# Layout of q, k and v prepared on the host for a fused attention and mixture-of-experts kernel

## The chip, the cores and the metric

The kernel runs on one core of a Trainium2 chip. The metric is the device time in microseconds of one execution, median of several runs. The core has a matmul engine (PE, with its weight loads PEld), a vector engine (DVE), a scalar engine (ACT), GpSimd (POOL), a queue engine that issues transfers (SP) and 16 DMA engines. Work that numpy does ahead of the launch is not part of the device time.

## The reference

Sparse attention over 8 batches, 8 heads, 576 positions, 64 per head, then a mixture of experts over the 4,608 tokens:

```
scores = scale * q @ k.T                       # scale = 1/8
mask_local   = (rel >= 0) & (rel < 32)         # heads 0..3, rel = query - key
mask_strided = (rel >= 0) & (key % 32 == query % 32)   # heads 4..7
x = softmax(where(mask, scores, -1e9)) @ v     # per head, heads side by side: 4608 x 512
noisy = x @ w_gate + log1p(exp(x @ w_noise)) * noise    # 8 experts
top2 of noisy, softmax weights over the two
out[t] += weight * (relu(x[t] @ w1[e]) @ w2[e])         # w1 512 x 1024, w2 1024 x 512
```

## The kernel before

Attention goes by units: one batch, one pair of heads, either local or strided, 32 units in all, four to a batch. A strided unit takes 72-key groups, a local unit 64 queries against 96 keys; each unit has nine blocks of 64 queries per head, worked in two items of four and five blocks.

A unit's steps, in the names of the code: `loads` (q, k, v by SP; the strided v passes through `vraw` and a copy into `v_s`, and its first 64 rows come a second time into `v_0`; the local v gets a column of ones in `v_l` and a copy of the 32 rows before each block, `front`); `prep` (L494 to L539: local q and k are reordered from `raw` to `ord` by a vector engine, transposed on PE in trains of three at L515, or of four at L519 for strided, and evacuated into `kT_l`, `qT_l`, `kT_s`, `qT_s`, q with the scale; strided units get a last block by eight quadrant copies); `products` (the masks as matmuls, L560, then the scores, L567); `item` twice (maximum `mx` L594, exponentials L598 and L600, transposes of them L608, evacuation to `aT`, values L627, for the fifth block of the second item L632, row sums, reciprocals and products L637 to L656 into `xo`); `finish` (stores of `xo` to `x_dram`, transposes L698 and L694, evacuation to `xT`). In the second item L632 writes the two heads of the fifth block side by side onto partitions 0 to 63.

After a batch's four units comes `route`: the gate matmul (L744), top two, and 12 scatters by POOL (L834) of the tokens' entries into a table in DRAM, `tab`. The experts work in jobs of two or three blocks of 128 tokens: table load by SP (L937), indices by POOL (L994), gathers of tokens from `x_dram` (L978, L985), transposes (L1020 on PE for early jobs, L1024 on DVE for others), a split into a high and a low part (cast L1031, subtraction L1033), layer 1 (L1062, twelve matmuls for each of eight parts of the hidden layer, then L1083 and L1088), layer 2 (L1114, 24 matmuls a block), `res` weighted (a ring of tiles), and a scatter with addition into `out` (L1150). Each expert's 16 weight tiles are loaded into `wraw` (five deep) and split by ACT (L904) and DVE (L905). Six jobs of experts 0 to 2 work on lists of the first 2, 3, 5 or 7 batches and can start while attention goes on; L1069 is one matmul on zeros ahead of some jobs. `out` is first filled with zeros by 12 transfers of 768 KB (L1199).

The order of everything is fixed when the program is built: each step is a `Piece` with an engine (or ANY, which is ACT or DVE), an estimated duration, a rank and what it reads and writes; `issue_all` places them one by one, each time the piece that can start first, and among those within 120 ns of it the one of lowest rank. A DMA waits in this plan until the planned wire is less than 5 us behind (zeros, `bulk`, 1.5 us); `t0` is the earliest planned time. On PE an expert's matmul is preferred while attention is ahead of it by PE time. Where the plan foresees an idle stretch of PE during attention it puts in matmuls on zeros (L375). Units have ranks 0, 10, 20 and so on; expert steps have ranks from `ER` = 1,000,000 on, so they come behind all attention that is ready. `near` is a hook for another rank and returns the rank itself:

```
def near(n, rank):

    return rank
```

Of the kernel before, what the change touches and what calls it, by code (L numbers as in the profile page):

```python
# [22 lines left out]
def kernel(  # L23
    ctx: ExitStack,
    tc: tile.TileContext,
    q: bass.AP,
    k: bass.AP,
    v: bass.AP,
# [7 lines left out]
    nc = tc.nc  # L36
    B, H, S, D = q.shape
# [5 lines left out]
    NP = HL // 2  # L43
# [8 lines left out]
    LP, LJ = S // 6, 6  # L52
# [109 lines left out]
    v_l = [keep.tile([KW, 2, NBL, D + 1], F32, name=f"v_l{i}") for i in range(2)]  # L162
    v_s = [keep.tile([G, 2, NJ, D + 1], F32, name=f"v_s{i}") for i in range(2)]

    v_0 = [keep.tile([G, 2, D + 1], F32, name=f"v_0{i}") for i in range(2)]
    xo_ = [keep.tile([128, 5, 2, D], F32, name=f"xo{i}") for i in range(3)]
    nc.vector.memset(kT_l[:, :STRIDE], 0.0)
    for i in range(2):
        nc.vector.memset(v_l[i][:, :, :, D:D + 1], 1.0)
        nc.vector.memset(v_l[i][:STRIDE, 0, 0, :], 0.0)  # L170
        nc.vector.memset(v_0[i][QB:], 0.0)
        nc.vector.memset(v_0[i][:QB, :, D:D + 1], 1.0)
        nc.vector.memset(v_s[i][:, :, :, D:D + 1], 1.0)
    nc.vector.memset(kT_s[:, NBL - 1, QB:], 0.0)
    for x in xo_:
        nc.vector.memset(x[QB:, 4, :, :], 0.0)
# [36 lines left out]

    PACE = 1.0
# [212 lines left out]
    for name, shape, dtype, depth in (  # L427
            ("raw", [LP, 2, LJ, D], F32, 2), ("ord", [LP, LJ, 2, D], F32, 1),
            ("vraw", [GP, NJ, D], F32, 1), ("ks", [GP, 2, NJ, D], F32, 1), ("qs", [GP, 2, NJ, D], F32, 1),
            ("mx", [128, 5], F32, 3), ("ex", [128, 5, KW], F32, 2), ("aT", [128, 5, 128], F32, 2),  # L430
            ("rs", [128, 6], F32, 2),
            ("xT", [128, S], F32, 5),
            ("noise", [TB, T, E], F32, 1), ("lsb", [TB, T, 2 * E], F32, 1), ("lgT", [96, S // 3], F32, 1),
            ("ns", [TB, T, E], F32, 1), ("nz", [TB, T, E], F32, 1), ("mv", [TB, T, 8], F32, 1),
            ("mi", [TB, T, 8], U32, 1), ("wt", [TB, T, 2], F32, 1), ("ixf", [TB, T, 2], F32, 1),
            ("oh", [TB, T, 2, E], F32, 1), ("ohs", [TB, T, E], BF16, 1),             ("cnt", [TB, E], F32, 1), ("addr_f", [TB, T, 2], F32, 1), ("ent", [TB, T, 2, 3], I32, 2), ("addr", [TB, T, 2], I32, 2)):
        R[name] = ring(keep, shape, dtype, name, depth)
    R["kT_l"], R["qT_l"] = Ring(1, fixed=[kT_l]), Ring(1, fixed=[qT_l])
    R["kT_s"], R["qT_s"] = Ring(1, fixed=[kT_s]), Ring(1, fixed=[qT_s])
    R["xo"] = Ring(3, fixed=xo_)  # L440
    R["v_l"], R["v_s"], R["v_0"] = Ring(2, fixed=v_l), Ring(2, fixed=v_s), Ring(2, fixed=v_0)

    def base_of(u):
        b, p, local = units[u]
        return (b * H + (2 * p if local else HL + 2 * p)) * S * D

    def loads(u, rank):

        base, local = base_of(u), units[u][2]
        res = {}  # L450

        def put(key, slot, parts, new):
            for i, (sel, src, off, dims, nbytes) in enumerate(parts):
                dma(lambda o, s=slot, sel=sel, src=src, off=off, dims=dims:
                    nc.sync.dma_start(sel(s.t), dram(src, off, dims)),
                    nbytes, rank, wires={D: 1.65, LJ * D: 1.2}.get(dims[-1][1], 1.0),
                    **({"alloc": [slot]} if i == 0 else {"write": [slot]}))
            res[key] = slot


        rows = GP if units[u][:2] != (B - 1, NP - 1) else G
        for key, src in (("k", k), ("q", q)):
            if local:
                put(key, R["raw"].new(), [(lambda t: t.rearrange("p h j d -> p h (j d)"), src, base,
                                           [[LJ * D, LP], [S * D, 2], [1, LJ * D]], 294912)], True)
            else:
                put(key, R[key + "s"].new(), [(lambda t: t[:rows].rearrange("p h j d -> p h (j d)"), src, base,
                                               [[NJ * D, rows], [S * D, 2], [1, NJ * D]], 4096 * rows)], True)
        if local:


            slot = R["v_l"].new()
            put("v", slot, [(lambda t: t[STRIDE:].rearrange("p h n d -> p (h n) d")[:, :, :D], v, base,
                             [[D, QB], [QB * D, 2 * NBL], [1, D]], 294912)], True)

            def front(o):
                vv = slot.t.rearrange("p h n d -> p (h n) d")
                copy(o.e, vv[:STRIDE, 1:, :D], vv[QB:, :2 * NBL - 1, :D])
            Piece("ANY", {"ACT": act(64 * (2 * NBL - 1)), "DVE": 760}, front, rank, read=[slot], write=[slot])
        else:  # L480
            slot = res["v"] = R["v_s"].new()
            for h in range(2):
                put(f"v{h}raw", R["vraw"].new(), [(lambda t: t[:rows].rearrange("p j d -> p (j d)"), v, base + h * S * D,
                                                   [[NJ * D, rows], [1, NJ * D]], 2048 * rows)], True)

                def spread(o, h=h, raw=res[f"v{h}raw"]):
                    copy(o.e, slot.t[:G, h, :, :D], raw.t[:G])
                Piece("ANY", {"ACT": act(NJ * D), "DVE": 420}, spread, rank, read=[res[f"v{h}raw"]],
                      **{"write" if h else "alloc": [slot]})
            put("v0", R["v_0"].new(),  # L490
                [(lambda t: t[:QB, :, :D], v, base, [[D, QB], [S * D, 2], [1, D]], 65536)], True)
        return res

    def prep(u, L, rank):  # L494

        local = units[u][2]
        kT, qT = (R["kT_l"].new(), R["qT_l"].new()) if local else (R["kT_s"].new(), R["qT_s"].new())
        tens = (("k", kT, None), ("q", qT, scale))
        for which, slot, factor in tens:
            for c in range(2):  # L500
                ps, src = Slot(), L[which]
                if local:

                    if c == 0:
                        L["o" + which] = R["ord"].new()
                        Piece("ANY", {"ACT": 840, "DVE": 75 + 0.62 * 768}, lambda o, src=src, dst=L["o" + which]: copy(
                            o.e, dst.t, src.t.rearrange("p h j d -> p j h d")), rank, read=[src], alloc=[L["o" + which]])
                    src = L["o" + which]

                def tr(o, c=c, ps=ps, src=src):  # L510
                    if local:

                        pv = ps.t[:, :S // 2].rearrange("r (x j) -> r j x", j=LJ // 2)
                        for j in range(LJ // 2):
                            nc.tensor.transpose(pv[:, j, :], src.t[:, LJ // 2 * c + j, :, :], ident[:LP, :LP])  # L515
                    else:

                        for j in range(NJ // 2):
                            nc.tensor.transpose(ps.t[:, G * j:G * j + G], src.t[:G, c, 2 * j:2 * j + 2, :], ident[:G, :G])  # L519
                Piece("PE", 260, tr, rank, read=[src], psum=ps)  # L520

                def evac(o, c=c, ps=ps, slot=slot, which=which, factor=factor):
                    if local:
                        dst = slot.t[:, STRIDE:] if which == "k" else slot.t.rearrange("r n x -> r (n x)")
                        dst = dst.rearrange("r (x j) -> r x j", j=LJ)[:, :, LJ // 2 * c:LJ // 2 * c + LJ // 2]
                    else:
                        dst = slot.t[:, 4 * c:4 * c + 4, :]
                    copy(o.e, dst, ps.t[:, :S // 2].rearrange("r (a b) -> r a b", b=LJ // 2 if local else G), factor)
                Piece("ANY", {"ACT": act(S // 2), "DVE": dve(S // 2)}, evac, rank, read=[ps],
                      **({"write" if c else "alloc": [slot]}))  # L530
        if not local:

            for _, slot, _ in tens:
                for c, r in enumerate(halves):
                    for odd, ro in enumerate(halves):
                        Piece("ANY", {"ACT": 240, "DVE": 205}, lambda o, slot=slot, c=c, r=r, odd=odd, ro=ro: copy(
# [761 lines left out]
```

## Time and profile before

| | |
|---|---|
| median of 3 runs | 1107.29 us (1105.77 to 1109.4) |
| profiled execution | 1117.46 us, span 1115.7 us |
| busy: PE, PEld | 1069.2 us (96%), 945.9 us (85%) |
| busy: DVE, ACT, POOL | 556.0 us (50%), 474.3 us (43%), 539.8 us (48%) |
| moved by DMA | 133.03 MB, mean 119 GB/s |

Times in rows are microseconds from the start of the span. An engine's busy time is the union of its instructions' records; a matmul's record goes on while the next one has started, so the step from start to start, not the length of a record, is what one costs in a train. A line of the form L515 is line 515 of the kernel before. The granted clock of PE (PEclk) is a share of 2.4 GHz; it has two levels, 1.2 and 2.4 GHz, and a figure between is a mean.

### The profile page before, as it was taken

To read this page: it belongs to the slowest core of one execution; us is meant where nothing else is said; L and a number is where in the kernel's file an instruction comes from. 1 tells how busy PE (TensorE), PEld (TensorE's weight loads), DVE (VectorE), ACT (ScalarE), POOL (GpSimd) and SP (SyncE) were. 2 spreads that over 40 slices of the span, in tenths; PEclk is the share of its full clock that TensorE was granted. 3 is DMA by queue.
4 is the path that set the end of the run, shared out by engine and by line. 5 is a ranking of instruction groups with operands and counts; after the bars stand their busy time and mean duration, and the time that the engine had idled before them with its cause. 6 is when DMAs were issued, how large, how long until landed. Compare 5 with 4: busy or idle time off the path is not lost.

```text
span 1115.7 us, 23537 instructions
## 1 busy us (share of the span) xinstructions
PE 1069.2 (96%) x8790; PEld 945.9 (85%) x8790; DVE 556.0 (50%) x1536; ACT 474.3 (43%) x1203; POOL 539.8 (48%) x661
## 2 busy tenths in 40 slices
PE   8988887989999999999999999999999999999997
PEld 7867766888788898988879898989989898989886
DVE  7857766865476224624746236323633462355231
ACT  6867766766565222423433224222512252244221
POOL 1044334423424467655668475646554655556432
PEclk9998989989999999999999999999999999999999
DMA  9986857878785134543555235523642363243222
GB/s 199 241 195 153 221 137 207 193 179 208 181 245 136 29 52 97 137 75 72 141 133 133 43 57 136 115 44 54 163 85 46 59 179 61 44 116 81 43 46 31
DMA packets 168430, 133.03 MB, mean 119 GB/s; under 512 B 51864, under 2 KB 136344, under 8 KB 168296
## 3 DMA queue, kind: packets, MB, share of 16 engines
q1 hardware_dynamic: 145160, 92.31, 32.1%
q0 software_dynamic: 23136, 38.94, 19.9%
q8 instruction: 83, 1.36, 0.5%
q14 instruction: 51, 0.42, 0.1%
HBM read 92.85 MB, written 39.39 MB: 119 GB/s over the span
## 4 chain that ended last, share of the span: by engine, by line
PE 87%; issue 5%; DVE 3%; DMA 1%; ACT 1%; POOL 1%; another core or an unknown queue 1%; POOLq 0%; SPq 0%; DVEq 0%; ACTq 0%
PE bankB L1114 6%; PE bankE L1114 5%; PE bankF L1114 5%; PE bankC L1062 5%; PE bankH L1062 5%; PE bankG L1062 5%; PE bankE L1062 5%; PE bankC L1114 5%; PE bankF L1062 4%; PE bankD L1062 4%; PE bankA L1062 4%; PE bankA L1114 4%; PE bankB L1062 4%; PE bankG L1114 4%; PE bankH L1114 3%
## 5 line engine op out<-in xcount | busy, mean ns | idle before, releaser
L985 POOL DMA_INDIRECT xg<-x_dram,gxx x248 | 258.5, 1043 | 165.8 <-DVE xr L1024 71.8
L1150 POOL DMA_INDIRECT out_dram<-res,tabt x80 | 133.4, 1667 | 99.7 <-ACT res L289 54.0
L834 POOL DMA_INDIRECT tab<-ent,addr x96 | 91.3, 951 | 89.9 <-issue 26.8
L1024 DVE STREAM_TRANSPOSE xr<-xg 128x512 f32<-128x512 f32 (+1 forms) x66 | 68.1, 1032 | 42.4 <-DMA xg<-x_dram,gxx 33.8
L1031 ACT CAST xhi<-xr 128x512 fp32r<-128x512 f32 (+1 forms) x66 | 39.1, 592 | 53.1 <-DVE xr L1024 51.2
L1033 DVE TENSOR_TENSOR xlo<-xr,xhi 128x512 fp32r<-128x512 f32 (+1 forms) x66 | 43.5, 659 | 35.9 <-ACT xhi L1031 25.2
L905 DVE TENSOR_TENSOR w1lo<-wraw,w1hi 128x512 fp32r<-128x512 f32 x80 | 54.5, 686 | 3.7 <-ACT w1hi L904 1.3
L905 DVE TENSOR_TENSOR w2lo<-wraw,w2hi 128x512 fp32r<-128x512 f32 x80 | 51.8, 684 | 1.2 <-ACT xT L288 0.7
L994 POOL TENSOR_SCALAR gix<-tabt 128x2 int32<-128x2 int32 (+1 forms) x32 | 8.0, 251 | 88.2 <-DMA tabt<-tab 71.0
L904 ACT CAST w1hi<-wraw 128x512 fp32r<-128x512 f32 x80 | 49.0, 618 | 0.4 <-DMA wraw<-in_moe_w_dram 0.2
L904 ACT CAST w2hi<-wraw 128x512 fp32r<-128x512 f32 x80 | 46.6, 617 | 3.3 <-DMA wraw<-in_moe_w_dram 2.7
L1062 PE MATMUL bankH<-xhi,w1hi 128*128 128x256 f32 (+3 forms) x132 | 40.5, 307 | 0.8 <-issue 0.8
L1062 PE MATMUL bankG<-xhi,w1hi 128*128 128x256 f32 (+3 forms) x132 | 40.0, 303 | 0.6 <-issue 0.6
L1062 PE MATMUL bankG<-xlo,w1hi 128*128 128x256 f32 (+3 forms) x132 | 39.4, 299 | 1.0 <-issue 1.0
L1062 PE MATMUL bankC<-xhi,w1hi 128*128 128x256 f32 (+3 forms) x132 | 39.8, 301 | 0.0
L1062 PE MATMUL bankH<-xhi,w1lo 128*128 128x256 f32 (+3 forms) x132 | 39.6, 300 | 0.0
L1062 PE MATMUL bankH<-xlo,w1hi 128*128 128x256 f32 (+3 forms) x132 | 39.6, 300 | 0.0
L1062 PE MATMUL bankG<-xhi,w1lo 128*128 128x256 f32 (+3 forms) x132 | 39.4, 298 | 0.0
L1062 PE MATMUL bankC<-xlo,w1hi 128*128 128x256 f32 (+3 forms) x132 | 39.1, 296 | 0.1
L1062 PE MATMUL bankC<-xhi,w1lo 128*128 128x256 f32 (+3 forms) x132 | 39.2, 297 | 0.0
L1114 PE MATMUL bankB<-w2hi,hhi 128*128 128x512 f32 x96 | 38.9, 405 | 0.0
L1062 PE MATMUL bankF<-xhi,w1hi 128*128 128x256 f32 (+3 forms) x128 | 38.2, 299 | 0.4 <-issue 0.4
(696 smaller groups left out, 3545.8 us busy)
## 6 DMA issues: line engine op xcount, KB each, us to landing
wraw<-in_moe_w_dram SPq DMA_DIRECT2D x160, 256.0 KB
out_dram<-zeros SPq DMA_DIRECT2D x12, 768.0 KB
ks<-in_k_dram SPq DMA_DIRECT2D x15, 320.0 KB
qs<-in_q_dram SPq DMA_DIRECT2D x15, 320.0 KB
vraw<-in_v_dram SPq DMA_DIRECT2D x30, 160.0 KB
raw<-in_k_dram SPq DMA_DIRECT2D x16, 288.0 KB
v_l<-in_v_dram SPq DMA_DIRECT2D x16, 288.0 KB
raw<-in_q_dram SPq DMA_DIRECT2D x16, 288.0 KB
```

The costliest lines, as they stand in the source:

```text
L834: st = nc.gpsimd.indirect_dma_start(out=tab, out_offset=bass.IndirectOffsetOnAxis(ap=s["addr"].t[:, t, kk:kk + 1], axis=0), in_=s["ent"].t ...
L904: Piece("ACT", 620, lambda o: nc.scalar.copy(hi.t, raw.t), rank, read=[raw], alloc=[hi], expert=True)
L905: Piece("DVE", 715, lambda o: nc.vector.tensor_tensor(lo.t, raw.t, hi.t.bitcast(F32), ALU.subtract), rank, read=[raw, hi], alloc=[lo], exp ...
L985: dma(lambda o, g=g: nc.gpsimd.indirect_dma_start(out=xg.t[:, g, :], out_offset=None, in_=x_dram[:4 * known, :], in_offset=bass.IndirectOf ...
L994: nc.gpsimd.tensor_scalar(gi.t[:, :nb], tb.t[:, :nb, 0], known - 1, None, op0=ALU.min)
L1024: Piece("DVE", 8.8 * rows, lambda o, xg=xg, xr=xr, ng=ng, rows=rows: nc.vector.transpose(xr.t.rearrange("p (c x) -> p c x", c=ND)[:, :, :r ...
L1031: Piece("ACT", 620 * rows // 128, lambda o, view=view, cols=cols: nc.scalar.copy(xh.t[:, :, cols], view()), rank, read=[xr], expert=True, ...
L1033: Piece("DVE", 725 * rows // 128, lambda o, view=view, cols=cols: nc.vector.tensor_tensor(xl.t[:, :, cols], view(), xh.t[:, :, cols].bitca ...
L1062: nc.tensor.matmul(ps.t[:, :width], a.t[:, 128 * d:128 * d + 128], c.t[:, d, :width], start=(m == 0), stop=(m == len(todo) - 1))
L1114: nc.tensor.matmul(ps.t, HT[n, f][p[0]].t[:, cols], W2[n][f][p[1]].t, start=(m == 0), stop=(m == len(todo) - 1))
L1150: st = nc.gpsimd.indirect_dma_start(out=out[:known, :], out_offset=bass.IndirectOffsetOnAxis(ap=places(), axis=0), in_=y.t[:rows, :], in_o ...
```

## The change

numpy lays out q, k and v ahead of the launch in the form of the kernel's tiles. For each batch and pair of heads, k and q of a local unit are transposed and put side by side (128 rows of 1,152), q and k of a strided unit likewise in the order of its blocks (128 rows of 1,216), v of either with its column of ones and, for strided, its first 64 rows as a ninth block. A unit has two transfers, `kq` and `v`; `prep` is gone, and the scale moves into the exponentials and one small step on `mx`. The fifth block's heads go to the two halves of the partitions, in the same PSUM tile as the others, with two copies into `xo` instead of one product. Rings: `mx` 5, `ex` 3, `aT` 3, `rs` 4 (before 3, 2, 2, 2), `res` 3 (before 4). Zeros get later `t0`, weights of the first expert earlier ones. Vector steps of early jobs, and the splits of their weights, get a rank after the batches of their list (`near`, with `LAG`).

```
-    kT_l = keep.tile([128, STRIDE + S], F32, name="kT_l")
-    qT_l = keep.tile([128, NBL, QB], F32, name="qT_l")
-    kT_s = keep.tile([128, NBL, G], F32, name="kT_s")
-    qT_s = keep.tile([128, NBL, G], F32, name="qT_s")
...
+    kq_t = [keep.tile([128, STRIDE + 2 * S], F32, name=f"kq_t{i}") for i in range(2)]
+    KS = 8 * G + QB
+    qk_t = [keep.tile([128, S + NBL * G], F32, name=f"qk_t{i}") for i in range(2)]
+    vt_l = [keep.tile([KW, 2, NBL, D + 1], F32, name=f"vt_l{i}") for i in range(2)]
+    vt_s = [keep.tile([GP, 2, NBL, D + 1], F32, name=f"vt_s{i}") for i in range(2)]
...
+    LAG = 60
...
         if local:
+            put("kq", "kq_t", lambda t: t[:, STRIDE:], kq_l, 128, 2 * S, rank)
+            put("v", "v_l", lambda t: t[STRIDE:].rearrange("p h n d -> p (h n d)"), v_l, QB, VW, v_rank)
...
+            put("kq", "qk_t", lambda t: t[:, :S + KS], qk_s, 128, S + KS, rank)
+            put("v", "v_s", lambda t: t.rearrange("p h n d -> p (h n d)"), v_s, GP, VW, v_rank)
...
-    def prep(u, L, rank):
...
-    def products(u, kT, qT, rank):
+    def products(u, kq, rank):
...
+                k0 = QB * blk if local else S + G * blk
+                q0 = (STRIDE + S if local else 0) + QB * blk
+                nc.tensor.matmul(sv[b][halves[half], s, :], kq.t[r, q0:q0 + QB], kq.t[r, k0:k0 + w], start=False,
...
+        Piece("DVE", 90, lambda o: nc.vector.tensor_scalar(mx.t, mx.t, scale, None, op0=ALU.mult), rank, write=[mx],
+              read=[mx])
...
-                nc.scalar.activation(exv()[:, n, :], view(sc)[:, n, :], AF.Exp, bias=mx.t[:, n:n + 1])
+                nc.scalar.activation(exv()[:, n, :], view(sc)[:, n, :], AF.Exp, bias=mx.t[:, n:n + 1], scale=scale)
...
-                    nc.tensor.matmul(extra()[:, h, :], aT.t[:w, 4, 64 * h:64 * h + 64], rhs, start=True, stop=True)
+                    nc.tensor.matmul(main(5)[64 * h:64 * h + 64, 4, :], aT.t[:w, 4, 64 * h:64 * h + 64], rhs, start=True,
+                                     stop=True)
...
-                nc.vector.tensor_tensor(xo.t[:QB, 4, :, :], extra()[:, :, :D],
-                                        rs.t[:QB, 4:, None].to_broadcast([QB, 2, D]), ALU.mult)
+        for h, r in enumerate(halves) if nb > 4 else ():
+            Piece("ANY", {"ACT": 270, "DVE": dve(D)}, lambda o, h=h, r=r: copy(
+                o.e, xo.t[:QB, 4, h, :], main(5)[r, 4, :D], rs.t[r, 4:5]), rank, read=[po, rs], write=[xo])
...
-                    nc.tensor.transpose(ps.t[:, :128], xo.t[:, 4, :, :], ident)
+                    nc.tensor.transpose(ps.t[:, :QB], xo.t[:QB, 4, :, :], ident[:QB, :QB])
...
-            ("res", [128, DM], F32, 4)):
+            ("res", [128, DM], F32, 3)):
...
-        dma(load, 262144, rank if turn is None else turn, alloc=[raw], expert=True, t0=70000 + 2000 * i)
-        Piece("ACT", 620, lambda o: nc.scalar.copy(hi.t, raw.t), rank, read=[raw], alloc=[hi], expert=True)
+        dma(load, 262144, rank if turn is None else turn, alloc=[raw], expert=True, t0=40000 + 1500 * i)
+        Piece("ACT", 620, lambda o: nc.scalar.copy(hi.t, raw.t), late or rank, read=[raw], alloc=[hi], expert=True)
...
         def near(n, rank):
 
-            return rank
+            hb = jobs[n][1][3]
+            return rank if hb == B else 20 * NP * hb + LAG
...
-            ER - 1, t0=26000 + 10000 * c + 35000 * (c >= 5), bulk=True))
+            ER - 1, t0=(90000, 130000, 170000, 230000, 270000)[(c > 2) + (c > 4) + (c > 7) + (c > 10)], bulk=True))
...
+def _laid_out(q, k, v):
...
+    def strided(a, g0):
+        x = pairs(a, H // 2)
+        y = x.reshape(B, NP, 2, G, NJ // 2, 2, D).transpose(0, 1, 5, 6, 2, 4, 3)[..., g0:]
+        return np.concatenate([y.reshape(B, NP, 2 * D, -1), turned(x[:, :, :, :QB])], -1)
...
+    return {"kq_l": np.concatenate([turned(pairs(k, 0)), turned(pairs(q, 0))], -1), "v_l": vl,
+            "qk_s": np.concatenate([strided(q, G - QB), strided(k, 0)], -1), "v_s": vs}
```

## Rows read from the trace of the kernel before

**Rows 1.** Stretch, length; busy PE, PEld, DVE, ACT, POOL (instructions); PEclk, DMA share, GB/s.

```profile
0.00:157.00 157.00, 137.94 (x2174) 112.16 (x2175) 111.89 (x457) 111.42 (x356) 45.40 (x115) 0.96 0.83 195
157.00:368.00 211.00, 197.18 (x2256) 170.34 (x2255) 135.13 (x483) 134.45 (x379) 78.17 (x128) 0.98 0.74 185
368.00:1104.00 736.00, 729.59 (x4345) 660.00 (x4345) 308.97 (x598) 227.74 (x468) 413.10 (x416) 1.00 0.40 85
1104.00:1116.00 12.00, 4.48 (x20) 3.38 (x18) 0.00 (x0) 0.69 (x1) 3.12 (x2) 0.78 0.35 49
```

**Rows 2.** The same view, the first units.

```profile
7.00:56.00 49.00, 46.38 (x801) 38.91 (x802) 41.10 (x160) 40.86 (x136) 1.60 (x5) 1.00 0.98 227
```

**Rows 3.** Timeline of PE: first and eighth unit's scores, batch 1's gate.

```profile
6.91 0.27 PE L567 MATMUL bankE<-kT_s,qT_s 64*64 64x72 f32 x1
...
58.40 0.24 PE L567 MATMUL bankC<-kT_l,qT_l 64*64 64x96 f32 x1
...
78.00 1.56 PE L744 MATMUL bankD<-xT,wg 128*32 128x192 f32 x24 [0.28 <-ACT v_s L288]
```

**Rows 4.** Timeline of POOL: batch 1's entries, its last scatter, indices of the first job.

```profile
85.77 0.20 POOL L822 COPY ent<-wt 96x12 f32<-96x12 f32 x1 [7.84 <-DVE wt L816]
...
111.00 0.91 POOL L834 DMA_INDIRECT tab<-ent,addr  x1 [1.50 <-ACT ex L598]
...
125.93 0.24 POOL L994 TENSOR_SCALAR gix<-tabt 128x2 int32<-128x2 int32 x1
```

**Rows 5.** Timelines of PE, ACT and DVE: the first job's first block.

```profile
136.99 0.65 PE L1020 MATMUL bankD<-ident,xg 128*128 128x128 f32 x4
...
140.24 0.58 ACT L1031 CAST xhi<-bankD 128x512 fp32r<-128x512 f32 x1
...
148.79 0.67 DVE L1033 TENSOR_TENSOR xlo<-bankD,xhi 128x512 fp32r<-128x512 f32 x1
...
156.79 0.37 PE L1062 MATMUL bankE<-xhi,w1hi 128*128 128x256 f32 x1
```

**Rows 6.** Timeline of PE where it never waits: trains of transposes.

```profile
265.21 0.41 PE L515 MATMUL bankD<-ident,ord 96*128 96x96 f32 x3
265.46 0.42 PE L519 MATMUL bankE<-ident,ks 72*128 72x72 f32 x4
265.71 0.41 PE L515 MATMUL bankC<-ident,ord 96*128 96x96 f32 x3
```

**Rows 7.** Stretch 0 to 157 us, line L515 alone, then L519 alone (PE, PEld).

```profile
0.00:157.00 157.00, 15.72 (x108) 10.61 (x108) 0.96 0.83 195
...
0.00:157.00 157.00, 15.15 (x152) 13.08 (x152) 0.96 0.83 195
```

**Rows 8.** Timeline of PE: values of four blocks, of the fifth, the next.

```profile
289.14 0.69 PE L627 MATMUL bankE<-v_s,aT 72*64 72x65 f32 x16
289.66 0.40 PE L632 MATMUL bankE<-v,aT 72*64 72x65 f32 x4
289.99 0.50 PE L1114 MATMUL bankA<-w2hi,hhi 128*128 128x512 f32 x1
```

**Rows 9.** Stretch 0 to 157 us, instructions of ord, kT_s and qT_s (PE, PEld, DVE, ACT).

```profile
0.00:157.00 157.00, 15.72 (x108) 10.61 (x108) 3.28 (x6) 10.80 (x13) 0.96 0.83 195
...
0.00:157.00 157.00, 9.80 (x324) 7.53 (x324) 5.79 (x21) 10.14 (x35) 0.96 0.83 195
...
0.00:157.00 157.00, 9.80 (x324) 7.53 (x324) 6.09 (x24) 9.64 (x31) 0.96 0.83 195
```

**Rows 10.** Line L375 alone in 0 to 157 us; timeline of one filler.

```profile
0.00:157.00 157.00, 20.21 (x137) 13.28 (x137) 0.96 0.83 195
...
31.96 0.82 PE L375 MATMUL bankD<-zeros 128*128 128x256 bf16 x6
32.62 0.62 PE L608 MATMUL bankD<-ident,ex 128*96 128x128 f32 x4
```

**Rows 11.** Timeline of SP: the second transfer of zeros.

```profile
63.08 0.60 SPq L1199 DMA_DIRECT2D out_dram<-zeros  x1
```

More of the change, by code (lines that the diff above doesn't have):

```diff
@@ L444, in base_of @@
         b, p, local = units[u]
[L445 to L468, printed above, removed]
@@ L492, in loads @@
-        return res
-    def prep(u, L, rank):
[L496 to L536, printed above, removed]
-                            o.e, slot.t[r, NBL - 1, :QB].rearrange("r (x j g) -> r j x g", j=NJ // 2, g=2)[:, :, :, odd],
-                            slot.t[ro, 4 * c:4 * c + 4, :QB // NJ]), rank, read=[slot], write=[slot])
-        return kT, qT
@@ L541, in products @@
-    def products(u, kT, qT, rank):
+                vv = slot.t.rearrange("p h n d -> p (h n d)")
+                copy(o.e, vv[:STRIDE, D + 1:], vv[QB:, :VW - D - 1])
+            Piece("ANY", {"ACT": act(VW - D - 1), "DVE": 760}, front, rank, read=[slot], write=[slot])
+        else:
+            put("kq", "qk_t", lambda t: t[:, :S + KS], qk_s, 128, S + KS, rank)
+            put("v", "v_s", lambda t: t.rearrange("p h n d -> p (h n d)"), v_s, GP, VW, v_rank)
+        return res
+    def products(u, kq, rank):
@@ L574, in scores @@
                 product(b, 4, b, NBL - 1)
-        o = Piece("PE", 20 + 10 * w / 4.8 + 5 * (188 if local else 144), scores, rank, read=[kT, qT], psum=sc)
+        o = Piece("PE", 20 + 10 * w / 4.8 + 5 * (188 if local else 144), scores, rank, read=[kq], psum=sc)
         o.order += in_turn[-1:]
@@ L891, with weights_of @@
     ZC = 384
-    def weights_of(e, layer, i, rank, turn=None):
+    def weights_of(e, layer, i, rank, turn=None, late=None):
         raw, hi, lo = R["wraw"].new(), R[f"w{layer}hi"].new(), R[f"w{layer}lo"].new()
@@ L1095, in lows @@
                     low(hh.t[:, width:width + tail], main, width)
-            Piece("DVE", dve(main) + (dve(tail) if tail else 0), lows, rank, read=[ps, hh], write=[hh] if tail else [],
+            Piece("DVE", dve(main) + (dve(tail) if tail else 0), lows, near(n, rank), read=[ps, hh], write=[hh] if tail else [],
                   alloc=[hl], expert=True)
@@ L1162, in experts @@
         for i in range(NF):
-            W[1, i] = weights_of(jobs[0][0], 1, i, ER, turn(0))
-        W2[0] = [weights_of(jobs[0][0], 2, i, ER, turn(0)) for i in range(NF)]
+            W[1, i] = weights_of(jobs[0][0], 1, i, ER, turn(0), near(0, ER))
+        W2[0] = [weights_of(jobs[0][0], 2, i, ER, turn(0), near(0, ER)) for i in range(NF)]
         transposes(0, ER)
@@ L1176, in experts @@
                 for i in range(NF):
-                    W[1, i] = weights_of(jobs[n + 1][0], 1, i, rank + 20, turn(n + 1))
+                    W[1, i] = weights_of(jobs[n + 1][0], 1, i, rank + 20, turn(n + 1), near(n + 1, rank + 20))
             if n + 1 < NJOB:
@@ L1184, in experts @@
                 if change:
-                    W2[n + 1] = [weights_of(jobs[n + 1][0], 2, i, rank + 21, turn(n + 1)) for i in range(NF)]
+                    W2[n + 1] = [weights_of(jobs[n + 1][0], 2, i, rank + 21, turn(n + 1), near(n + 1, rank + 21)) for i in range(NF)]
         Piece("POOL", 7000, lambda o: nc.gpsimd.drain(), rank, after=[out_done[E - 1][-3]], expert=True)
```

137 lines of the change are left out of this document (60 added, 77 removed).

## Prediction

> **What bounds the kernel now.** I read the stretches first: four stages, cut where the first expert matmul starts (157 us), where the last attention work ends (368) and where the last matmul ends [rows 1]. Stage A, 0 to 157 us, has attention and routing alone; stage B, 157 to 368, mixes attention with the jobs of experts 0 to 2 whose tokens are already routed; from 368 on there are expert jobs alone. The reader is to see the idle time of PE: 19.1 us in A (157 less 137.9), 13.8 in B, 6.4 in the 736 us behind, and a tail. From 157 us on the kernel is bound by the sum of PE's work. A change can gain in two ways only: less PE work anywhere, or a shorter stage A, where PE waits and where part of its busy time is filler (matmuls on zeros, L375, that the planner puts into gaps it foresees).
>
> Then I read what sets the length of A. In its first third DMA, DVE and ACT are all near their ends: 98% share, 41.1 and 40.9 of 49 us [rows 2]. The eighth unit, the last of batch 1, has its scores at 58.4 us, the first at 6.9: 7.4 us a unit; batch 1's gate follows at 78.0 [rows 3]. From there a chain of small steps leads to the first expert job: entries ready at 85.8, the twelfth scatter at 111.0, indices at 125.9 on POOL [rows 4]; the tokens' first block is transposed at 137.0, but its cast on ACT comes at 140.2, its subtraction on DVE at 148.8, and the first expert matmul at 156.8 [rows 5]. The expert's vector steps have the lowest rank and stand behind attention. So A = 78 us to the gate + 79 us of routing and preparation.
>
> **The change part by part.** *Transposes of q and k (prep).* In a stretch where PE never waits, trains of these transposes start 0.25 us apart [rows 6]. There are 128 trains (32 units, two tensors, two halves): 128 x 0.25 = 32.0 us of PE work gone. Their summed busy time is higher (an instruction's record overlaps the next one's start), so 32 is the value; 0.42 us, a train's own length in the same rows, bounds it at 53. In A 36 + 38 = 74 trains run [rows 7], so 18.5 us of it lies there and 13.5 in B.
>
> *The fifth block's values.* Its four matmuls (a head's fp32 product counts as two) write the same partitions and take 0.33 us, while 16 ordinary ones, in pairs on opposite halves, take 0.52 [rows 8], or 0.13 for four. After the change the two heads write opposite halves: 0.20 saved in 32 units, 6.4 us (bounds 0, if they don't overlap, and 10.6). The small transpose L694, now 64 by 64: half of a transpose, 0.06 us in 32 units, 2 us (bounds 0 and 4). Together 40.4 us of PE work: 18.5 + 3.4 (17 units) + 1 = 22.9 in A, 17.5 in B.
>
> *Vector work.* Gone are the reordering of raw, the evacuations to kT and qT, the quadrant copies and the spread of v. The three largest groups alone held ACT for 30.6 and DVE for 15.2 us of A [rows 9]. Added are two scalings of mx a unit and one copy more for the fifth block; the nearest rows are those of kT_s, copies of more elements, at a mean of 0.28 on DVE (5.79 us for 21): at most 0.84 us a unit, 15 in A, against 46 gone. So the two engines end below their present 111 of 157 us each [rows 1], and PE and DMA set the pace. The memsets removed lie in the first 7 us, under the loads.
>
> *Loads.* Bytes stay (1.88 MB for two units, by the shapes; the padding adds under 1%), seven transfers become four, runs of 256 to 2,048 bytes become 4.6 to 4.9 KB. DMA moved 227 GB/s at 98% share [rows 2]; 0.94 MB in and 0.29 MB out make 5.4 us a unit. A gain in rate isn't shown here, so none is the lower bound.
>
> *Pace.* PE's kept work bounds a unit from below: stage A's 137.9 less 22.9 less filler of 15.1 (137 at 0.11; six start 0.66 us ahead of their successor, [rows 10]) is 99.9 us for 18.5 units, 5.4. Unchanged is 7.4. I take the middle, 6.3: the eighth scores at 6.9 + 7 x 6.3 = 51. The Trainium skill (DMA: Bandwidth & Descriptors, section Bandwidth) says that efficiency grows with a transfer's size, with 138 GB/s at 64 KB and 341 at 1 MB; no row here shows its rate for the merged transfers. By an estimate from that page a unit's traffic would need 3.6 us, the pace would fall to PE's 5.4, and the forecast by 6 us.
>
> *Gate and routing.* The gate follows the eighth scores by 19.6 us now; with fewer steps to queue behind I take 16 (bounds 12 and 19.6): 67. Routing keeps 7.8 us to the entries and about 23 for the scatters (26 now; POOL is unchanged, its pacing follows the vector engines). Table load and indices, 14 now, 12; gather, 11 now, 9. From the first transposes to the first expert matmul took 19.8 us; the steps that waited now have rank 40 x 2 + 60 = 140, ahead of units 14 and up, and at 115 us those are the units in work: 5 us (the steps' own 0.6 + 0.7 us twice, and the hops). Sum 56.8, first expert matmul at 124 instead of 157.
>
> *Price of the ranks.* Expert casts now go ahead of attention steps on both engines: attention units 14 and up wait behind them. Cover is expert PE work that is ready by then; without it the price is the 1.3 us of cast and subtraction per tile, 16 tiles per expert. I take 0.
>
> *Weights earlier, zeros later.* Of the twelve transfers of zeros the planner let the first go at 26 us or later, and the second left at 63.1 [rows 11], in A's loaded part; now none goes before 90 in the planner's time. One costs 3.5 us at 227 GB/s. The weights' start moves from 70 to 40 us and takes the room: 0 net. Scatters into out wait for zeros on POOL, and with res three deep instead of four a late zero would hold a PSUM bank. The first scatter of a list of three batches needs five transfers of zeros: bounds 0 and their 17 us, if they all have to go then.
>
> *Sum.* In A the filler and idle are 157 - 99.9 - 22.9 = 34.2; with A at 124 and the same attention work done 124 - 99.9 = 24.1. So A gives 22.9 + 10.1 = 33.0, B 17.5, the rest 0: 50.5 us. The profiled execution took 1117.5 us (span 1115.7), 10.2 above the median of the runs shown, 1107.3. 1117.5 - 50.5 - 10.2 = 1056.8: **1057 us**.
>
> **The rivals.**
> *1, forecast:* 1040 to 1072, which is A at 107 to 139. Chance 0.55.
> *2, A collapses further.* With the pace at 5.4 and the gate 12 us behind, the first expert matmul comes at about 105: 19 us less, 1038. For it: all three loaded resources of rows 2 are relieved at once. Against it: the scatter chain of POOL isn't, and DMA still carries the same bytes. Chance 0.17.
> *3, A keeps its length.* If loads, or the scatters, set it anyway, the work removed there turns into idle time and filler, and only B's 17.5 remain: 1107 - 17.5 = 1090. For it: DMA at 98%, and in B it must move in some 150 us what took 211 at a share of 0.74 [rows 1], which gives 1.04 if nothing is postponed. Against it: zeros can slip behind 368, where the share is 0.40. Chance 0.20, most of it between 1072 and 1090.
> *4, nothing happens:* attention shorter but routing chain and expert supply as late, PE's saving filled by zeros: 1107. From 157 us on PE has no filler to grow, so only 0.03.
> *5, slower.* PE's granted clock. The mean of 0.96 in A and 0.98 in B [rows 1] means 12.6 + 8.4 = 21 us at half speed already. With transposes gone PE has less to do ahead of the first expert job; should the clock stay at 1.2 GHz, t us of it lose up to t/2 of work. The 50.5 us are lost at 101 us more, 122 in all: nearly the whole of A at 124 us. For it: PE fell to half in A and B although filled. Against it: the filler remains and the density of work rises (99.9 of 124, against 122.8 of 157). The Trainium skill (TensorE: Matmul & The Clock Gate, Part 1: The HAM clock gate) holds that the slow level is the default and sustained activity ends it; the falls in stages A and B and none to speak of behind 368 (1.00) agree. Chance 0.05, other ways to lose included.
>
> **How the numbers follow.** The likeliest is 1, so 1057. The range leaves out the low third of 2 (below 1030, 0.05), the upper end of 3 (above 1085, 0.06), 4 and 5 (0.08): 0.19, so 1030 to 1085. The measurement of this kernel can tell 0.3%, 3.3 us, from no change. Faster: 1, 2 and 3, 0.92. Same: 4, 0.03. Slower: 5, 0.05.
>
> **What the changed profile would show.** PE busy time less by 40 us besides filler, with no line of transposes of q and k; the first expert matmul near 124; cast, subtraction and matmul within some 5 us of the first token transposes; attention over near 315 or before; DMA's share in what remains of B above 0.85; behind it the same PE-bound stage with 6 us idle. Wrong I would be if the scores of the eighth unit still came at 58 (loads bind), if the gap from gate to first expert matmul stayed near 79 (POOL binds), if stage B had more than 20 us of idle PE (the vector ranks, zeros or loads starve it), or if the expert matmuls' own time changed, which nothing in the trace speaks for.

## The result, and the profile after

The changed kernel takes 1073.4 us (median of 4 runs, 1070.1 to 1076.7) against 1106.5 (1105.0 to 1109.4): a ratio of 0.970, 95% interval 0.966 to 0.974. The forecast was 1057, in a range of 1030 to 1085. The gain is 33 us where 50.5 were worked out. Chips differ: the kernel before takes 1106 to 1114 us on some and 1065 on others, so each experiment is compared with the kernel before on its own chip.

The stretches of the profiled execution (1074.0 us, span 1071.9), cut at the same events as [rows 1]:

```profile
0.00:145.00 145.00, 130.02 (x2046) 98.86 (x2046) 92.76 (x396) 94.89 (x298) 46.43 (x115) 0.95 0.79 216
145.00:305.00 160.00, 153.14 (x1874) 128.49 (x1875) 102.67 (x372) 88.55 (x273) 65.02 (x120) 0.98 0.76 199
305.00:1064.00 759.00, 756.02 (x4494) 685.48 (x4493) 320.34 (x616) 238.03 (x487) 423.05 (x425) 1.00 0.43 91
1064.00:1072.00 8.00, 0.43 (x2) 0.00 (x1) 0.00 (x0) 0.69 (x1) 1.56 (x1) 0.73 0.30 43
```

Stage A shrank from 157 to 145 us, B from 211 to 160; the last stage grew, since more of the expert jobs lie in it. PE is still idle for 15.0 us of A, and for 6.9 in B and 3.0 behind.

PE's timeline has the eighth unit's scores, batch 1's gate and the first expert matmul (answering [rows 3] and [rows 5]):

```profile
45.10 0.24 PE L483 MATMUL bankH<-kq_t 64*64 64x96 f32 x1
...
66.31 0.51 PE L655 MATMUL bankF<-xT,wg 128*32 128x192 f32 x4
...
144.62 0.36 PE L974 MATMUL bankH<-xhi,w1hi 128*128 128x256 f32 x1
```

The eighth scores come 13 us earlier, the gate 12 and the first expert matmul 12: from the gate on nothing was won. Where the 78 us from the gate to the first expert matmul go is seen on POOL (entries, last scatter, indices; [rows 4]) and on PE, ACT and DVE (first block; [rows 5]):

```profile
74.67 0.20 POOL L733 COPY ent<-wt 96x12 f32<-96x12 f32 x1 [4.61 <-DVE wt L727]
...
100.59 0.92 POOL L745 DMA_INDIRECT tab<-ent,addr  x1 [0.22 <-issue]
...
121.68 0.24 POOL L906 TENSOR_SCALAR gix<-tabt 128x2 int32<-128x2 int32 x1
```

```profile
138.72 0.90 PE L932 MATMUL bankC<-ident,xg 128*128 128x128 f32 x4
...
139.65 0.59 ACT L943 CAST xhi<-bankC 128x512 fp32r<-128x512 f32 x1
...
141.85 0.65 DVE L945 TENSOR_TENSOR xlo<-bankC,xhi 128x512 fp32r<-128x512 f32 x1
```

The last step, transposes to matmul, fell from 19.8 to 5.9 us, as the ranks ask. But indices came 21.1 us behind the last scatter (14.9 before) and the transposes 17.0 behind the indices (11.1 before). In POOL's timeline six scatters of the next batch now stand between the last scatter and the indices; before there was one. And PE's filler has grown, in the same view as [rows 10], from 137 matmuls to 208:

```profile
0.00:145.00 145.00, 29.31 (x196) 18.31 (x196) 0.95 0.79 216
145.00:305.00 160.00, 1.87 (x12) 1.29 (x12) 0.98 0.76 199
```

### The profile page after: what moved, and what is told of

Read it like the earlier page. It is cut to its first block, busy times and chain, and to the rows that moved or that the text cites. A ratio compares the mean times of both kernels' runs of the same rounds, so it can differ in the third digit from the quotient of the medians.

```text
span 1071.9 us, 22349 instructions
## 1 busy us (share of the span) xinstructions
PE 1039.6 (97%) x8413; PEld 912.8 (85%) x8413; DVE 515.8 (48%) x1383; ACT 422.1 (39%) x1059; POOL 536.0 (50%) x661
## 3 DMA queue, kind: packets, MB, share of 16 engines
q0 software_dynamic: 23136, 38.94, 21.2%
## 4 chain that ended last, share of the span: by engine, by line
PE 89%; issue 5%; DVE 3%; ACT 2%; POOL 1%; another core or an unknown queue 1%; POOLq 0%; ACTq 0%; DVEq 0%
PE bankC L1026 5%; PE bankD L974 5%; PE bankF L1026 5%; PE bankB L974 5%; PE bankH L974 5%; PE bankD L1026 5%; PE bankE L974 5%; PE bankE L1026 5%; PE bankA L974 5%; PE bankG L974 4%; PE bankG L1026 4%; PE bankF L974 4%; PE bankC L974 4%; PE bankB L1026 4%; PE bankH L1026 4%
## 5 line engine op out<-in xcount | busy, mean ns | idle before, releaser
L897 POOL DMA_INDIRECT xg<-x_dram,gxx x248 | 255.9, 1032 | 177.2 <-DVE xr L936 76.2
L733 POOL COPY ent<-wt 96x12 f32<-96x12 f32 x8 | 3.1, 392 | 86.0 <-DVE wt L727 86.0
L974 PE MATMUL bankD<-xhi,w1hi 128*128 128x256 f32 (+3 forms) x132 | 40.7, 308 | 0.5 <-issue 0.5
L974 PE MATMUL bankB<-xhi,w1hi 128*128 128x256 f32 (+3 forms) x136 | 41.0, 301 | 0.0
L974 PE MATMUL bankB<-xlo,w1hi 128*128 128x256 f32 (+3 forms) x136 | 40.2, 295 | 0.6 <-issue 0.6
L974 PE MATMUL bankB<-xhi,w1lo 128*128 128x256 f32 (+3 forms) x136 | 40.4, 297 | 0.2
L974 PE MATMUL bankD<-xhi,w1lo 128*128 128x256 f32 (+3 forms) x132 | 39.7, 301 | 0.0
L974 PE MATMUL bankD<-xlo,w1hi 128*128 128x256 f32 (+3 forms) x132 | 39.6, 300 | 0.0
L974 PE MATMUL bankH<-xhi,w1lo 128*128 128x256 f32 (+3 forms) x132 | 39.3, 298 | 0.0
L974 PE MATMUL bankA<-xhi,w1hi 128*128 128x256 f32 (+3 forms) x128 | 38.2, 299 | 0.7 <-issue 0.7
L974 PE MATMUL bankE<-xhi,w1hi 128*128 128x256 f32 (+3 forms) x128 | 38.2, 298 | 0.0
```

The lines of the kernel that those rows point to most:

```text
L733: nc.gpsimd.tensor_copy(s["ent"].t[:, :, :, 1].bitcast(F32), s["wt"].t)
L897: dma(lambda o, g=g: nc.gpsimd.indirect_dma_start(out=xg.t[:, g, :], out_offset=None, in_=x_dram[:4 * known, :], in_offset=bass.IndirectOf ...
L974: nc.tensor.matmul(ps.t[:, :width], a.t[:, 128 * d:128 * d + 128], c.t[:, d, :width], start=(m == 0), stop=(m == len(todo) - 1))
```

## The experiments

**Both kernels again, on one chip whose clock holds.**

> The kernel before, unedited, to see on one chip what its profile shows when the granted clock does not fall: the first four experiments ran on a chip where it was 0.997 or more and the kernel before took 1064.6 us, not 1106.5. Theory 1 (what differs between the chips is the clock in the two attention stages and what it delays): the granted clock is 0.995 or more, the expert-only stage lasts as long as before (736 us, within 8), and the first 368 us shrink by 30 or more. Theory 2 (all stages run faster on that chip): the expert-only stage shrinks by 20 us or more.

> The changed kernel, unedited, as the measure for all the others on one chip. Theory 1 (the first expert matmul at 144.6 instead of the 124 forecast came from the falls of the clock and late vector steps behind them): with a clock of 0.995 or more the first expert matmul comes at 122 to 130, and the ratio to the kernel before is 0.969 to 0.975. Theory 2 (the routing chain over POOL and SP takes 78 us by its program order): it comes at 138 or later again.

Measured: 1065.3 and 1033.4 us, ratio of the changed kernel 0.971 (0.969 to 0.973). Stretches of the kernel before, cut at its first expert matmul, the end of attention and the last matmul, then its filler; below, the same of the changed kernel:

```profile
0.00:136.00 136.00, 127.63 (x2170) 105.64 (x2171) 111.41 (x454) 110.38 (x355) 47.94 (x115) 1.00 1.00 219
136.00:325.00 189.00, 186.97 (x2256) 163.89 (x2253) 136.13 (x485) 135.02 (x378) 79.82 (x128) 1.00 0.87 211
325.00:1055.00 730.00, 730.00 (x4377) 662.22 (x4371) 311.25 (x599) 230.70 (x469) 414.74 (x417) 1.00 0.41 86
...
0.00:1100.00 1100.00, 20.21 (x137) 13.25 (x137) 1.00 0.55 121
```

```profile
0.00:124.00 124.00, 117.59 (x2042) 91.49 (x2043) 93.55 (x396) 93.71 (x295) 48.33 (x115) 1.00 0.91 252
124.00:270.00 146.00, 145.58 (x1879) 124.32 (x1877) 104.32 (x372) 89.69 (x277) 65.50 (x120) 1.00 0.87 221
270.00:1023.00 753.00, 753.00 (x4496) 684.05 (x4496) 323.15 (x616) 240.62 (x487) 423.18 (x425) 1.00 0.43 92
...
0.00:1100.00 1100.00, 30.03 (x208) 19.13 (x208) 1.00 0.52 121
```

The gate and the first expert matmul, in the kernel before and then in the changed one:

```profile
71.03 0.36 PE L744 MATMUL bankD<-xT,wg 128*32 128x192 f32 x3
...
136.21 0.36 PE L1062 MATMUL bankE<-xhi,w1hi 128*128 128x256 f32 x1
```

```profile
62.28 0.53 PE L655 MATMUL bankF<-xT,wg 128*32 128x192 f32 x6
...
124.31 0.37 PE L974 MATMUL bankH<-xhi,w1hi 128*128 128x256 f32 x1
```

The first 368 us of the kernel before shrink by 43 here (325), the expert-only stage by 6: its theory 1. The changed kernel's first expert matmul comes at 124.3, so theory 1 there too. That this is the 124 of the forecast is chance: the forecast starts from 156.8, and on this chip the kernel before has its own at 136.2, so A shrinks by 12 us on either chip. From the gate to the first expert matmul it takes 65 us before and 62 after: the change shortens the chain by 3 us.

This pair gives the account of the gain. The engines' busy time, before and after:

```profile
PE 1045.0 (98%) x8790; PEld 931.7 (88%) x8790; DVE 558.8 (53%) x1536; ACT 476.8 (45%) x1203; POOL 544.1 (51%) x661
...
PE 1016.4 (99%) x8413; PEld 899.8 (87%) x8413; DVE 521.0 (51%) x1383; ACT 424.7 (41%) x1059; POOL 538.6 (52%) x661
```

The spans differ by 32.2 us (1062.8 and 1030.6). PE's busy time fell by 28.6, although filler grew by 9.8: other work fell by 38.4. Idle time went from 17.8 to 14.2. So -38.4 + 9.8 - 3.6 = -32.2.

**PE work put back, by stage.**

```diff
+            for i in range(10 if u < 18 else 0):     # the other kernel: u >= 18
+                nc.tensor.matmul(sc[0].t[:, :256], warm[:, :128], warm, start=True, stop=True)
+        o.dur += 1070 * (u < 18)
```

> The changed kernel with ten matmuls on zeros (128x256, 0.107 us each, 1.07 us a unit) put in front of the scores of each of the first 18 units, 19.3 us of PE work in all, about what the transposes of q and k cost there; the planner knows of them. Theory 1 (ahead of the first expert matmul the routing chain sets the length and PE's saved work has turned into filler): filler falls from 27 us by 10 or more, the first expert matmul stays within 5 us of 144.6, the time rises by 0 to 8 us, 1073 to 1081. Theory 2 (the PE sum rules in this stage too): the first expert matmul comes 12 to 19 us later and the time rises by 15 to 19 us, 1088 to 1093.

> The same ten matmuls in front of the scores of the last 14 units, 15.0 us of PE work, in the stage that mixes attention and expert jobs. Theory 1 (from the first expert matmul on the time is the sum of PE's work): the time rises by 12 to 16 us, 1085 to 1090. Theory 2 (this stage waits for the supply of expert work, so the work hides in its idle time): the time rises by 0 to 6 us, idle time of PE between 145 and 305 us, 7 us now, goes to nothing.

Measured: 1040.0 us, ratio 0.975 (0.972 to 0.979), and 1048.7, ratio 0.984 (0.980 to 0.988), where the changed kernel has 0.971. In the first, the busy time of the filler, that of the added matmuls, all engines' busy time, and the first expert matmul:

```profile
0.00:1100.00 1100.00, 19.01 (x139) 13.00 (x139) 1.00 0.52 121
...
0.00:1100.00 1100.00, 23.38 (x180) 18.26 (x180) 1.00 0.52 121
...
PE 1027.4 (99%) x8524; PEld 910.1 (88%) x8524; DVE 516.9 (50%) x1367; ACT 428.0 (41%) x1075; POOL 535.6 (52%) x661
...
133.41 0.36 PE L977 MATMUL bankF<-xhi,w1hi 128*128 128x256 f32 x1
```

Of some 23 us of work put into the first 18 units, 11.0 replaced filler (30.0 to 19.0) and 2.0 idle time; the span (1039.6) grew by 9.0, the ratio by 0.005, about 5 us. The ratios' intervals touch, but all four runs (1039.3 to 1041.4 us) lie above the slowest changed kernel of the pair (1035.5). In the last 14 units 17.6 us cost a ratio of 0.013, 14 us; PE's busy time there shows the same:

```profile
PE 1032.2 (99%) x8544; PEld 912.1 (87%) x8544; DVE 518.5 (50%) x1382; ACT 427.9 (41%) x1060; POOL 539.9 (52%) x661
```

This is 15.8 us above the 1016.4 of the changed kernel, and the span is 15.7 above. Theory 1 holds for both, but for one point: in the former the first expert matmul came at 133.4, 9 us behind the 124.3 of the pair, and not within 5. What PE saves is worth nearly its full length behind the first expert matmul, and a fifth to two fifths of it ahead (5 to 9 of 23).

The first of these runs also splits the gain, since it has nearly the old amount of PE work ahead of the first expert matmul. Its span is 23.2 us under that of the kernel before: PE's work other than filler is 16.4 less, filler 1.2 and idle time 5.6 less. The changed kernel's is another 9.0 us shorter. So of the 32.2 us some 16 are PE work behind, 9 are PE work ahead, and 7 are filler and idle time that the other edits spare (less vector work, other loads, ranks, rings); these were not taken apart beyond the ranks below. The spans are of two chips whose clock holds; the medians of this chip alone give 24.6 us for the 23.2.

**Other parts taken back.** Layout alone, and ranks alone taken back:

```diff
 def near(n, rank):
-    return rank if hb == B else 20 * NP * hb + LAG
+    return rank
-    t0=40000 + 1500 * i                                   # layout alone: this and the next, too
+    t0=70000 + 2000 * i
-    t0=(90000, 130000, 170000, 230000, 270000)[...]
+    t0=26000 + 10000 * c + 35000 * (c >= 5)
```

> The changed kernel with three of its edits taken back: the expert's vector steps keep their low ranks, the weights start at 70 us and later, the zeros at 26 us and later, as in the kernel before; the laid-out q, k, v stay. Theory 1 (the time is the sum of PE's work plus the filler and idle time ahead of the first expert matmul): the PE work removed stays removed, some 39 us; from the first token transposes to the first expert matmul it takes some 20 us again instead of 5.9, so the first expert matmul comes at 155 to 160 instead of 144.6, and a part of these 10 to 15 us is lost: 1079 to 1087. Theory 2 (the layout only moves work that was hidden; ranks and starts of the transfers carry the gain): 1095 to 1107. Theory 3 (ranks and starts are worth nothing): 1070 to 1077.

> The changed kernel with only the ranks taken back (the expert's vector steps stand behind those of attention again). Theory 1 (when the first expert matmul comes does not matter, as PE finds as much attention work in its place; ranks are worth nothing): from the first token transposes to the first expert matmul it takes 20 us or more, and the time stays within 3 us of the changed kernel. Theory 2 (ranks gain what zeros and weights lose): the time rises by 6 to 15 us.

Measured: 1035.8 us, ratio 0.973 (0.968 to 0.977), and 1036.8, ratio 0.973 (0.972 to 0.975). First token transposes and first expert matmul of the layout alone, then of the kernel without ranks:

```profile
116.08 0.63 PE L932 MATMUL bankD<-ident,xg 128*128 128x128 f32 x3
...
154.10 0.37 PE L974 MATMUL bankA<-xhi,w1hi 128*128 128x256 f32 x1
```

```profile
116.75 0.51 PE L932 MATMUL bankH<-ident,xg 128*128 128x128 f32 x2
...
134.51 0.36 PE L974 MATMUL bankD<-xhi,w1hi 128*128 128x256 f32 x1
```

The layout alone (with it the fifth block and the depths of the rings) has 29 of the 32 us. Its first expert matmul comes 30 us later than the changed kernel's, and this costs 2 us, no more than the measurement can tell: attention runs ahead in the meantime (the last unit's scores begin at 226 instead of 244 us), and PE has the same sum of work (1017.4 us busy for 1016.4). Without the ranks it takes 17.8 us from the first transposes to the matmul instead of 5.6; they are worth 3.4 us on the same chip, a little more than the spread of the runs. The starts of zeros and weights, what is left between the two experiments, show no worth, within some 5 us.

**The routing chain shortened.** Scatters of batch 2 behind the first job's gathers, and the table load planned 4 us closer:

```diff
+    for x in scatters[2]:
+        x.order += first_rows
-                    far=4000, **how)
+                    far=0 if n == 0 else 4000, **how)
```

> The changed kernel with the third batch's scatters on POOL put behind the first job's indices and its first two gathers, and the first job's table load planned 4 us closer behind the last scatter. Theory 1 (the routing chain over POOL and SP is what sets the first expert matmul): it comes at 128 to 138 instead of 144.6, and the time falls by 3 to 6 us, to 1067 to 1070, as about 30% of that stage is filler and idle time. Theory 2 (loads or vector steps of attention set it): the first expert matmul moves by less than 4 us and the time stays within 3 us of 1073.

Measured: 1035.0 us, ratio 0.971 (0.967 to 0.975). The edit did not do what it was meant to:

```profile
104.37 0.24 POOL L907 TENSOR_SCALAR gix<-tabt 128x2 int32<-128x2 int32 x1 [6.38 <-DMA tabt<-tab]
108.60 1.04 POOL L891 DMA_INDIRECT xg<-x_dram,gix  x1 [3.99 <-DVE rs L553]
```

The indices came 3.9 us earlier than the 108.3 of the changed kernel, the gather only 0.2 (108.60 for 108.79), as it waits for a vector step: the planner ties a POOL transfer to one that it has placed shortly before. The table load left SP at 99.6 us (99.7 in the changed kernel), 10 us behind the last scatter, among stores of attention's output that wait for their data. The first expert matmul moved by 0.8 us. So this run says nothing on the worth of a shorter chain; the layout alone and the kernel without ranks, where it is longer, do.

**No filler, and half of it.**

```diff
-                for i in range(int((room - 150) // 150)):
+                for i in range(0):                        # half: // 300
```

> The changed kernel without the filler that the planner puts into gaps (208 matmuls on zeros, 27 us); nothing of the computation is left out. Theory 1 (filler stands where PE would wait for loads and vector steps anyway): the time stays within 3 us, idle time of PE grows by 20 us or more. Theory 2 (filler delays real work): the time falls by 8 to 25 us. Theory 3 (filler keeps the granted clock up): the clock falls to half in stretches ahead of the first expert matmul that had none, and the time rises by 5 us or more.

> The changed kernel with about half of the filler (one matmul on zeros for each 300 ns of a foreseen gap instead of 150). Theory 1 (half is enough for the clock, and the other half only took time from real work): the granted clock stays at 1.00 ahead of the first expert matmul, and the time falls by 2 to 6 us. Theory 2 (all of it stands in real gaps and the clock holds): within 2 us. Theory 3 (the clock falls in places): the time rises by 2 to 8 us, less than the 9 us without any filler.

Measured without filler: 1042.3 us, ratio 0.978 (0.976 to 0.980), 8.9 us more than the changed kernel on the same chip: its theory 3. The stretch ahead of 124 us:

```profile
0.00:124.00 124.00, 103.18 (x1650) 79.22 (x1650) 84.79 (x357) 84.41 (x265) 42.08 (x103) 0.83 0.86 228
```

The mean clock there is 0.83 instead of 1.00, that is a third of the stretch at 1.2 GHz; 26 us of filler (counted from one start to the next) are gone, idle time grew by 16 (to 30.2), and the rest of PE's work took 23 us longer, which makes the 12.9 by which this span (1043.5) is longer. So, by estimate, 16 of the 26 us of filler stood in gaps that are there without it. Half of the filler gave 0.966 (0.961 to 0.970) on one of the chips where the clock falls, with a mean clock of 0.978 in the profiled run and 0.90 in A: a ratio lower than the changed kernel's 0.970 by 0.4%, which the intervals don't tell apart, so none of its theories is borne out whole.

**What makes the gaps.** Three tries: the planner's rate, the loads, the softmax's maximum.

```diff
-    RATE = 245.0
+    RATE = 300.0
```

```diff
-  dma(... dram(src, n * rows * width, [[width, rows], [1, width]])), 4 * rows * width, ...)
+  few = rows if u < 4 else 2
+  dma(... dram(src, n * rows * width, [[width, few], [1, width]])), 4 * few * width, ...)
```

```diff
-        Piece("DVE", dve(5 * w), lambda o: nc.vector.tensor_reduce(mx.t, view(sc), AX.X, ALU.max, negate=True), ...)
-        Piece("DVE", 90, lambda o: nc.vector.tensor_scalar(mx.t, mx.t, scale, None, op0=ALU.mult), ...)
```

> The changed kernel with one number of the planner changed: it reckons with 300 GB/s for transfers instead of 245. Theory 1 (the filler comes from gaps that the planner foresees behind transfers it takes for slow): filler falls by 4 us or more, loads leave earlier, and the time falls by 2 to 8 us. Theory 2 (the transfers are no faster for it): less filler turns into idle time of PE, the time stays within 2 us or rises, and the granted clock may fall where filler is gone.

> The changed kernel with the loads of q, k and v cut to two rows of each tile from the fifth unit on (attention there works on what the tiles held), some 26 MB of transfers less; the planner knows. Everything else is as it was. Theory 1 (transfers set the pace of attention ahead of the first expert matmul, so PE's saved work has turned into filler): filler falls from 26 us to 15 or less, units 8 to 18 follow each other by 5.5 us or less instead of 7.0, and the time falls by 8 to 20 us below the changed kernel's 1033. Theory 2 (the vector steps and hops between engines set it): filler stays at 20 us or more and the time within 4 us.

> The changed kernel without the row maximum of the softmax: its reduction and its scaling on VectorE (0.54 + 0.13 us, two of each a unit, 43 us in all) are left out and the exponential takes the scores unshifted, which gives the same weights for scores as small as these. Theory 1 (the chain of steps between PE, DVE and ACT sets the pace ahead of the first expert matmul, and so how much of PE's saved work turns into filler and idle time there): units 8 to 18 follow each other faster by 0.7 us or more, filler falls by 5 us or more, and the ratio to the kernel before falls from 0.970 to 0.955 to 0.965. Theory 2 (transfers or the program order set it): filler and ratio stay within 3 us of the changed kernel's.

Measured: the rate 0.971 (0.964 to 0.977), no change, with 188 fillers for 208 (theory 2). Tiny loads 0.958 (0.954 to 0.962), 13 us below the changed kernel's ratio. Scores of the eighth and the eighteenth unit, and the filler:

```profile
45.99 0.24 PE L484 MATMUL bankF<-kq_t 64*64 64x96 f32 x1
...
130.51 0.24 PE L484 MATMUL bankD<-kq_t 64*64 64x96 f32 x1
```

```profile
0.00:1100.00 1100.00, 25.96 (x186) 17.16 (x186) 0.99 0.44 97
```

Ten units in 84.5 us, 8.5 each, though DMA's share up to 124 us is only 0.53; the changed kernel took 8.3 (45.1 to 128.3) in its first profile, on a chip of the same kind. Loads don't set the pace there, and filler is above 20 us: theory 2 on these points, theory 1 on the time. Some 4 us of the 13 are not the loads': other attention results route tokens otherwise, and 16 of 1,792 second-layer matmuls (0.23 us each) fell away. Some 3 more, by estimate, are the clock: its profile has 10 us at half speed between the first and the last matmul, that of the other rate, on the same chip, 17. The rest isn't explained. Without the maximum, 0.965 (0.962 to 0.968), 5 us less, which the interval of the first result (0.966 to 0.974) hardly tells apart; the same rows:

```profile
39.09 0.24 PE L483 MATMUL bankD<-kq_t 64*64 64x96 f32 x1
...
141.43 0.24 PE L483 MATMUL bankG<-kq_t 64*64 64x96 f32 x1
```

```profile
0.00:1100.00 1100.00, 29.09 (x188) 18.13 (x188) 0.98 0.52 121
```

The first eight units come faster (4.8 us each for 5.6), the next ten slower (10.2 for 8.3), and the filler stays: neither theory. The comparison is loose: in this profile, from another chip, PE stood still for 21.7 us with nothing to wait for that the profile shows, against 13.3 in the first profile.

## Why the prediction was right, and where it was off

**The time.** 1073.4 lies in the stated range, but 1.4 us outside of rival 1's own stretch (1040 to 1072), at the near end of rival 3's.

**The bound.** Right: from the first expert matmul on, the time is the sum of PE's work (17.6 us put back cost 14).

**PE work removed, 40.4 us.** Measured 38.4 on the chip whose clock holds, 40.6 in the profiles of the first chip (busy time 1069.2 to 1039.6, filler 20.2 to 31.2). On the former chip, counted from one start to the next, the transposes of q and k held 35.8 us (forecast 32.0), the fifth block went from 10.7 to 6.4 (4.3 for 6.4), and the small transpose won nothing (4.9 to 6.6). So the sum is nearer than its terms.

**Filler and idle time, 34.2 to 24.1 us.** This is the step that failed. It took them as what is left of a stage A of 124 us once the kept work, 99.9, is done, so that A would give all of PE's saving there and 10.1 us on top. On the pair whose clock holds, filler grew by 9.8 and idle time fell by 3.6: +6.2 for -10.1. Of the 18.3 us between 50.5 and 32.2 this is 16.3, and the PE work is the other 2.0. In stage A on the first chip the two together went from 39.3 us (20.2 of filler, 19.1 idle) to 44.3 (29.3 and 15.0). What the runs showed in its place: more than half of what PE saves ahead of the first expert matmul turns into filler or idle time (13.0 of the 23 us put back), and the other edits take only 6.8 of that off again. That is the half of rival 3 that came true; the other half, a stage A of its old length, did not.

**Gate at 67 us.** 66.3, but by luck, as two errors cancel: the pace is 5.6 us a unit, not 6.3, and the gate follows the eighth scores by 21.2, not 16. The pace is close to PE's 5.4. DMA moved more at a lower share, in the first 28 us of the two kernels on the chip whose clock holds (first before, then changed):

```profile
0.00:28.00 28.00, 24.62 (x356) 19.81 (x356) 20.62 (x85) 19.31 (x57) 4.64 (x31) 1.00 0.99 203
```

```profile
0.00:28.00 28.00, 26.38 (x442) 20.57 (x442) 16.21 (x65) 17.98 (x57) 4.63 (x31) 1.00 0.91 283
```

203 GB/s became 283. That larger transfers run more efficiently is what the Trainium skill (DMA: Bandwidth & Descriptors, section Bandwidth) says; here the trace agrees. Two units' transfers went from eight of 32 to 320 KB (the forecast counted seven) to four of 293 to 608 KB, and their runs became longer too, so the trace doesn't say which of the two did it. The 6 us that a pace of 5.4 would have taken off the forecast did not show in the time.

**Routing, 56.8 us.** 78.3 in the first profile (entries 8.4, scatters 25.9, indices 21.1, transposes 17.0, matmul 5.9), 62.0 on the chip whose clock holds, where it was 65 before. Of the terms the entries (7.8) and the last one (5) were about right, the three between too short. But the price of this miss is small: a first expert matmul 30 us later cost 2 us. The chain was the wrong thing to count in.

**Ranks, 0.** They gain 3.4 us. **Zeros, weights, res: 0.** Zeros and weights: right; the shallower ring of results wasn't tried alone.

**The clock (rival 5).** It did not fall further (0.987 for 0.986), with more filler than before. Without filler it does. The Trainium skill (TensorE: Matmul & The Clock Gate, Part 1: The HAM clock gate) holds the slow level for the default that sustained activity ends; the run without filler agrees, with 0.83 in A.

**Signs.** One sign of being wrong came: the gap from gate to first expert matmul stayed at 78.3 ("near 79"). It was read as POOL setting the time, and the layout-alone run speaks against that. The others did not come: the eighth scores at 45.1 and not 58, idle time in B 6.9 (under 20), and the experts' two layers the same (826.5 us before and 824.1 after on the chip whose clock holds, from start to start). Attention was over at 305 (forecast 315 or before), and 3.0 us were idle behind (6). DMA's share in B was 0.76 and not above 0.85; on the chip whose clock holds it was 0.87, as before the change.

**The profiled execution.** It was 10.2 us above the median before and 0.6 after, so the two first profiles differ by 43.8 us in span, the medians by 33; taking the 10.2 off was right.

**Open.** What makes the gaps that the planner fills in A: neither loads nor the maximum's vector steps nor the planner's rate alone removes them. And which of the other edits spares the 7 us of filler and idle time.

## What to carry to other kernels

Work taken off the bounding engine is worth its length only where that engine is the bound in the stage at hand: split the sum by stage, and in a stage with filler or waits price it at a fraction (here a fifth to two fifths) until a run with dummy work put back says more. An early stage's landmark, such as the first expert matmul, is no measure of time when the engine has other work for the meantime. And compare profiles of both kernels from one chip.

## What the hardware showed

Between chips the same program differed by 4%: the changed kernel took 1073.4 and 1033.4 us. In the changed kernel's first profile, on the slower kind, the granted clock fell to half in five stretches ahead of 500 us (24 us in all), and PE stood still with nothing to wait for that the profile shows ("issue"): 26 times, 13.3 us in all, against once on the other chip. Three of the 14 such groups in the view of PE's waits on the first (total, times, longest):

```profile
PE bankB L483 <- issue: 2.0, 5, 0.4
PE bankG L483 <- issue: 2.0, 3, 1.0
PE bankD L483 <- issue: 1.8, 3, 1.1
```

and the one on the other:

```profile
PE bankB L543 <- issue: 0.3, 1, 0.3
```

The two together are some 25 of the 40 us (half of 24, and 13); the rest, and what makes the gaps, wasn't found. The gain of the change is the same on both kinds: 33 and 32 us.
